# An FFT convolution's last tile: its scratch in four parts instead of three, two of them reloaded early, and 20 filler matmuls instead of 18

## The chip, the core and the metric

The kernel runs on one core of a Trainium2 chip. The metric is the device time of one execution in microseconds, lower is better. The core has five engines with their own instruction streams: TensorE (PE, matmuls; PEld are its weight loads), VectorE (DVE), ScalarE (ACT), GpSimd (POOL) and SyncE (SP), which here only issues transfers. A transfer (DMA) runs on 16 DMA engines beside them and can be issued from SP or from ACT (SPq and ACTq in the profile).

## What is computed

```python
def reference(x, w):                       # x [1, 224, 224, 96], w [7, 7, 96, 96], bf16
    B, H, W, C = x.shape
    K = w.shape[0]
    wp = jnp.pad(w, ((0, H - K), (0, W - K), (0, 0), (0, 0)))
    Xf = rfft2(x.astype(float32), axes=(1, 2))
    Wf = rfft2(wp.astype(float32), axes=(0, 1))
    Yf = jnp.einsum('bhwi,hwio->bhwo', Xf, Wf)
    return irfft2(Yf, s=(H, W), axes=(1, 2)).astype(bfloat16)
```

That is a circular convolution of a 224 x 224 image of 96 channels with a 7 x 7 filter.

## The kernel before

The image is cut along its height into 8 bands of 28 rows (`NJ`, `B`) and along its width into 7 tiles of 32 columns (`t` = 0 to 6; the last is `TL`). Along the height the kernel uses a short transform of 34 points per band, which gives 17 frequencies (`NS`), each with a real and an imaginary part. Every tile goes through three stages, which are interleaved instruction by instruction:

- A: the transform of the columns of the next tile, into `xf` (matmuls pb<-Fm,xn).
- B: for each frequency s = 0 to 16 a round (`b_round`) of matmuls with the transformed filter `WF`, whose results VectorE, ScalarE and GpSimd combine into `yf`. Three frequencies (two at the end) make one group of `yf`, and each group is put to a scratch tensor in DRAM (`scr`), because the next stage needs its rows in another order of partitions. In the last tile the puts of all groups but the last are issued from ACT, one round or so after their sums (`puts`, line 705), the last one from SP.
- C: the inverse transform. The scratch is loaded back with the frequencies of two or three bands on the partitions (`tt`), multiplied with the matrix `G`, evacuated from PSUM to `yo` and written to the output. In the rounds of a tile, jobs of the C stage of the tile before it are interleaved (`c_jobs`, `CQ`, `pace`). Outputs of the next to last tile (except one kind) are kept back in the list `outs` and issued behind the late loads (lines 769 and 984).

After the last tile's rounds there is nothing left to interleave with, so its C stage is cut in two along the frequencies. `SLAST = (0, 9, 15, 17)` (line 37) names the parts. Part 0 (frequencies 0 to 8, tensor `scra`) is loaded back early, in two transfers of 64 and 8 rows at round s = 11 (lines 971 to 975), into `tl_a`, 72 partitions (`KA`). The parts 1 and 2 (frequencies 9 to 14 and 15 to 16, tensors `scrb`) are loaded by `load_b` (line 732) once their puts have landed, 96 and 32 rows of `tl_b`, 128 partitions. Both lie in a buffer of `xf` that is free by then. The matrices for them, `GA` (4 bands at once) and `GB`, are copied together from `G` by small transfers in the tiles 3 and 4 (`g_parts`, line 735; one at each round, line 970).

The end of the kernel (lines 977 to 1016) is then, in program order: the six C jobs left over of tile 5; both `load_b`; the outputs in `outs`; eight early products (`first`, with `GA` and `tl_a`) into the eight PSUM banks; `WARM` = 18 filler matmuls of zeros, which add nothing to the last of these banks (line 1002); then sixteen times a late product (`second`, with `GB` and `tl_b`) onto an early one, its evacuation by VectorE or ScalarE, and after every second an output of 168 KB. The other eight early products follow as banks come free.

SP issues its transfers in program order, and waits in place where a transfer needs something that is not there yet. All helpers record their instructions at one line (L99), so the profile is read by tiles: `xf<-scra` is the early reload, `xf<-scrb` the late loads, `scra<-yf` and `scrb<-yf` the puts of the last tile, `pb<-xf,GA` the early products, `pb<-wu` at the end the fillers, `pb<-xf,GB` the late products.

Of the kernel before, what the change touches and what calls it, by code (L numbers as in the profile page):

```python
# [8 lines left out]
BF16 = mybir.dt.bfloat16  # L9
# [5 lines left out]
B = 28  # L15
# [5 lines left out]
NJ = 8  # L21
# [3 lines left out]
TW = 16  # L25
# [8 lines left out]
PGRP = ((0, 5), (5, 8), (8, 11), (11, 14), (14, 17))  # L34
YGRP = ((0, 3), (3, 6), (6, 9), (9, 12), (12, 15), (15, 17))
YGRPL = ((0, 3), (3, 6), (6, 9), (9, 12), (12, 15), (15, 17))
SLAST = (0, 9, 15, 17)
SA = SLAST[1]
YMAX = 3
YBUF = 4  # L40
JGB = ((0, 3), (3, 6), (6, 9), (9, 12), (12, 15), (15, 17))
# [4 lines left out]
SH3 = (0, 8, 17)  # L46
MERGE = ()
NP2 = 0
WARM = 18
HEAD = ("w",) * 6 + ("x0", "w", "w", "h0", "h1", "w", "w", "x1", "w", "w")  # L50
W1 = 30
ZC = 48
# [12 lines left out]
def kernel(  # L65
# [7 lines left out]
    _, H, W, C = x.shape  # L73
    assert tuple(w.shape) == (KT, KT, C, C) and C == 96 and H == NJ * B and W % (2 * TW) == 0
    NT = W // (2 * TW)
    TL = NT - 1
# [29 lines left out]
    VE, SE, GE, TE, DE = (_Ordered(e) for e in (nc.vector, nc.scalar, nc.gpsimd, nc.tensor, nc.sync))  # L106

    cpool = ctx.enter_context(tc.tile_pool(name="const", bufs=1))
    dr_pool = ctx.enter_context(tc.tile_pool(name="scr", bufs=4, space=bass.MemoryType.DRAM))
# [30 lines left out]
    def tail_evac(out_ap, in_ap, n):  # L140
        cv, ca = 75 + 1.25 * n, 85 + 1.03 * n
        if load["v"] + cv <= load["a"] + ca:
            load["v"] += cv
            return VE.tensor_copy(out=out_ap, in_=in_ap)
        load["a"] += ca
        return SE.copy(out=out_ap, in_=in_ap)

    def dma(out_ap, in_ap):
        return DE.dma_start(out=out_ap, in_=in_ap)
# [7 lines left out]
    G = cpool.tile([3 * FR, 3 * B], BF16, name="Gm")  # L157
    KA = 4 * 2 * SA
    NL = len(SLAST) - 1
    KB = [NJ * 2 * (SLAST[i + 1] - SLAST[i]) for i in range(1, NL)]  # L160
    RB = [sum(KB[:i]) for i in range(NL - 1)]
    assert sum(KB) == 128
    XW = 2 * TW * C
    xn_all = [cpool.tile([128, XW + 32], BF16, name=f"xn{i}") for i in range(2)]
    xn_bufs = [xb[0:R] for xb in xn_all]
# [366 lines left out]
    def a_jobs(t):  # L532
        xf = new_xf(t)
        jobs = []
        for jg in range(2):
            for h in range(2):
                for (q, n) in ((0, 3), (3, 3), (6, 2)):
                    jobs.extend(a_bank(t, xf, xn_bufs[jg], h * PXC + 2 * q, n, jg, HALO + h * 8 + q))
            jobs.append(then_load(jobs.pop(), t + 1, jg))
        return jobs  # L540
# [23 lines left out]
    def jit(t, g):  # L564
        s0, s1 = JGB[g]
        n = s1 - s0
        xf = xf_tiles[t][0:C]
        xv = xf.rearrange("c p r s w j -> c p r s (w j)")
        b = jcount[0] % 3 if t < 2 else (jcount[0] - 2 * len(JGB)) % 2
        jcount[0] += 1  # L570
        Jb = J_bufs[b][0:C].rearrange("c (k s q) -> c k s q", k=7, s=3)
        for s in range(s0, s1):
            jbuf[(t, s)] = Jb[:, :, s - s0]

        def sub(o, a, b, op, cost):
            def f():
                load["v"] += 170 + cost / 1.92
                return VE.tensor_tensor(out=o, in0=a, in1=b, op=op)
            return f
        x0, x1 = xv[:, 0, :, s0:s1], xv[:, 1, :, s0:s1]  # L580
        c0, c1 = max(s0, REAL[0] + 1), min(s1, REAL[1])
        i0, i1 = c0 - s0, c1 - s0
        pd, rd, sd, qd = x1.ap
        dpl = bass.AP(x1.tensor, x1.offset - NJ, [pd, [NJ, 2], rd, sd, qd])
        cuts = ((0, 1), (1, n)) if t == g == 0 else ((0, n),)
        return [
            sub(Jb[:, 0:4, a:b].rearrange("c (k r) s q -> c k r s q", r=2), dpl[:, :, :, a:b],
                x0[:, :, a:b].unsqueeze(1).to_broadcast([C, 2, 2, b - a, PP]), ALU.subtract, 4 * PP * (b - a)) for a, b in cuts] + [
            sub(Jb[:, 4, i0:i1], xv[:, 0, 0, c0:c1], xv[:, 0, 1, c0:c1], ALU.add, PP * (c1 - c0)),
            sub(Jb[:, 5:7, i0:i1], Jb[:, 0:4:2, i0:i1], Jb[:, 1:4:2, i0:i1], ALU.add, 2 * PP * (c1 - c0)),  # L590
        ]
# [13 lines left out]
    def b_round(t, s, mid, end, ydve=False, planes=()):  # L605
# [90 lines left out]
        if s == y1 - 1:  # L696
            dst, yo0 = scr_tiles[t], 0
            if t == TL:
                i = sum(s >= v for v in SLAST[1:])
                dst, yo0 = scr_tiles[(t, i)], SLAST[i]  # L700

# [8 lines left out]
    scr_tiles = {}  # L710
# [18 lines left out]
    tl_a = tl_all[0:KA, 0:2 * TW2].rearrange("p (w g e) -> p w g e", g=2, e=2 * C)  # L729
    tl_b = tl_all[:, 2 * TW2:3 * TW2].rearrange("p (w e) -> p w e", e=2 * C)  # L730

    def load_b(i):
        dma(tl_b[RB[i]:RB[i] + KB[i]], scr_tiles[(TL, 1 + i)].rearrange("w j s (r e) -> (j s r) w e", r=2))

    def g_parts():
        for j in range(4):
            dma(GA[j * 2 * SA:(j + 1) * 2 * SA, j * B:(j + 1) * B], G[0:2 * SA, 0:B])
            yield
        for j in range(NJ):
            for i in range(NL - 1):  # L740
                s, s1 = SLAST[i + 1:i + 3]
                n = 2 * (s1 - s)
                dma(GB[RB[i] + j * n:RB[i] + (j + 1) * n, j // 4, j % 4 * B:(j % 4 + 1) * B], G[2 * s:2 * s1, 0:B])
                yield
# [59 lines left out]
    outs = []  # L804
# [9 lines left out]
    def queue_c(t):  # L814
        pend.extend((t, *k) for k in (LT if t < TL - 1 else LTL))
        pump()
# [33 lines left out]
    def fills(qs, k):  # L850
        def f():
            for q in qs:
                pace(q, k)
        return f
# [3 lines left out]
    def add(a, b, jobs):  # L858
        qs.append([a, b, jobs, len(jobs)])
# [15 lines left out]
    for r in range(NS + LAG):  # L875
# [28 lines left out]
        if r == PGRP[-2][1] + 1:  # L904
# [6 lines left out]
            GA = g_pool.tile([KA, 4 * B], BF16, name="GA")  # L911
            GB = g_pool.tile([128, 2, 4 * B], BF16, name="GB")
# [4 lines left out]
        for t in range(2):  # L917
            s = r - LAG * t
# [11 lines left out]
    if NP2:  # L930
# [3 lines left out]
        pools["ps"], pools["psb"] = (c.__enter__() for c in ps_cms)  # L934
    cj = c_jobs(0)
    gp = g_parts()
    for t in range(2, NT):
        if t == TL:
            scr_tiles[t] = None
            scr_tiles[(t, 0)] = dr_pool.tile([TW, NJ, SA, 4 * C], BF16, name="scra")  # L940
            for i in range(1, NL):
                scr_tiles[(t, i)] = dr_pool.tile([TW, NJ, SLAST[i + 1] - SLAST[i], 4 * C], BF16, name=f"scrb{i}")
        else:
            scr_tiles[t] = dr_pool.tile([TW, NJ, NS, 4 * C], BF16, name="scr")
        qs = []
        if t + 1 < NT:
            add(4 if t == 2 else 0, 26, a_jobs(t + 1))
        nold, nnew = CQ[t]
        k1 = 2 * NS if t < TL else 2 * NS - 8
        k0 = {2: 15, TL: 6}.get(t, 3)  # L950
        km = k0 + -(-(k1 - k0) * nold // (nold + nnew))
        add(k0, km, cj[:nold])
        cn = c_jobs(t - 1)
        cj = cn[nnew:]
        add(km, k1, cn[:nnew])
        plan = {}
        for g, (s0, s1) in enumerate(JGB):
            if g + 1 < len(JGB) or t + 1 < NT:
                plan[s0 if g + 1 < len(JGB) else s0 - 1] = g
        for s in range(NS):  # L960
            now = ()
            if s in plan:
                g = plan[s]
                now = jit(t, g + 1) if g + 1 < len(JGB) else jit(t + 1, 0)
            if s == 2 and t == 2:
                queue_c(0)
            if s == (3 if t in (2, TL) else 2):
                queue_c(t - 1)
            if t in (3, 4):
                next(gp, None)  # L970
            if t == TL and s == SA + 2:
                sv = scr_tiles[(TL, 0)].rearrange("w (g j) s (r e) -> (j s r) (w g) e", g=2, r=2)
                ta = tl_a.rearrange("p w g e -> p (w g) e")
                for p0, p1 in ((0, KA // 16 * 16), (KA // 16 * 16, KA)):
                    dma(ta[p0:p1], sv[p0:p1])
            b_round(t, s, fills(qs, 2 * s), fills(qs, 2 * s + 1), bool(now) if t < TL else s % 3 == 2 or s >= NS - 3, now)
    tail[0] = 1
    load["v"], load["a"] = 1000.0, 0.0
    while cj:
        cj.pop(0)()  # L980
    assert not pend
    for i in range(NL - 1):
        load_b(i)
    for f in outs:
        f()
# [6 lines left out]
    def first(g, q):  # L992
        pc = bank()[0:M4, 0:4 * C]
        TE.matmul(pc.rearrange("p (w e) -> p w e", w=2), lhsT=GA[:], rhs=tl_a[:, 2 * q:2 * q + 2, g], start=True, stop=False)
        return pc

    def second(g, q, pc, yo):
        TE.matmul(pc, lhsT=GB[:, g], rhs=tl_b[:, 2 * q:2 * q + 2, :].rearrange("p w e -> p (w e)"), start=False, stop=True)
        tail_evac(yo[0:M4, q % 4 * 4 * C:(q % 4 + 1) * 4 * C], pc, 4 * C)
    order = [(g, q) for h in range(2) for g in range(2) for q in range(4 * h, 4 * h + 4)]  # L1000
    live = {k: first(*k) for k in order[:8]}
    for _ in range(WARM):
        TE.matmul(live[order[7]].rearrange("p (a b) -> p a b", a=3), lhsT=wu[:, 0:M4], rhs=wu[:].unsqueeze(1).to_broadcast([128, 3, 128]),
                  start=False, stop=False)
# [44 lines left out]
```

## Time and profile before

| What | Value |
|---|---|
| Time, median of 3 runs | 264.14 us (263.65 to 265.39) |
| The profiled execution's own time | 263.5 us |
| Its span, first to last instruction | 261.8 us |
| TensorE busy | 251.5 us (96%) |
| VectorE busy | 220.1 us (84%) |
| ScalarE busy | 196.7 us (75%) |
| GpSimd busy | 97.3 us (37%) |
| Mean granted TensorE clock | 0.992 |

Times inside the profile are microseconds from the span's start. The profile has a page of totals and answers to queries: a chain of work that ended last (from the last instruction back, at each step to what released it), a timeline in order of time (start, duration, engine, output<-input, how many instructions are merged, and in brackets the idle time before and who ended it), lists of waits, and windows (busy time of each engine in a stretch, the granted TensorE clock as a share of full speed, the busy share of the DMA engines and GB/s). Matmuls are pipelined, so a matmul's duration is longer than the distance to the next one's start.

### The profile page before, as it was taken

The numbers are of one execution on the slowest core, as the hardware profiler recorded it, in microseconds if no ns is written. First come the engines' busy times: TensorE is split into PE (matmuls) and PEld (weight loads), VectorE is DVE, ScalarE is ACT, GpSimd is POOL, SyncE is SP. The second block draws the span as 40 slices with busy tenths as digits, with TensorE's granted clock in tenths as the row PEclk, the third lists the DMA queues.
The fourth block names the chain that finished last, engine by engine and source line by source line (L and its number), as shares of the span: only waits on it lengthen the run. The fifth ranks groups of instructions, "written<-read, shape, count | busy, mean of one in ns | idle before, by whom it ended". The sixth has DMA issues, their size and how long they took to land.

```text
span 261.8 us, 11952 instructions
## 1 busy us (share of the span) xinstructions
PE 251.5 (96%) x5046; PEld 232.7 (89%) x5046; DVE 220.1 (84%) x462; ACT 196.7 (75%) x470; POOL 97.3 (37%) x152
## 2 busy tenths in 40 slices
PE   8999999999999999999999999999999999999793
PEld 3979999999989999989999998999999999989561
DVE  6889998899999789868887788788988799999623
ACT  8979978697745967988988799887988852654422
POOL 7783224464655622241223412333134423325000
PEclk9999999999999999999999999999999999999889
DMA  7994105511112698987967496979688442877796
GB/s 177 272 195 126 48 6 155 161 49 48 48 51 85 185 251 155 296 265 192 274 188 218 120 265 207 241 209 357 241 171 248 135 136 87 221 206 212 177 276 195
DMA packets 46889, 46.77 MB, mean 179 GB/s; under 512 B 35308, under 2 KB 38064, under 8 KB 46836
## 3 DMA queue, kind: packets, MB, share of 16 engines
q1 hardware_dynamic: 46116, 44.54, 62.1%
q10 hardware_dynamic: 720, 1.47, 1.7%
q8 instruction: 39, 0.64, 1.1%
q14 instruction: 14, 0.11, 0.1%
HBM read 24.66 MB, written 21.33 MB: 176 GB/s over the span
## 4 chain that ended last, share of the span: by engine, by line
PE 76%; DMA 11%; DVE 8%; issue 2%; ACT 1%; SPq 1%; DVEq 0%; ACTq 0%
PE pb L99 75%; DVE J L99 3%; DMA xn<-in_x_dram 3%; DMA WF<-in_x_dram 3%; DMA xf<-scrb 2%; DVE WF L99 2%; DMA wq<-in_w_dram 2%; DMA scrb<-yf 1%; PE ps L99 1%; DVE v L99 1%; DVE yf L99 1%; DVE u L99 1%; SPq L99 1%; ACT WF L99 0%; DVE tt L99 0%
## 5 line engine op out<-in xcount | busy, mean ns | idle before, releaser
L99 PE MATMUL pb<-WF,J 96*128 96x96 bf16 x2821 | 162.4, 206 | 1.7 <-DVE J L99 0.7
L99 PEld LDWEIGHTS <-J 96*128 96x128 bf16 x2821 | 137.9, 98 | 10.6 <-issue 3.5
L99 POOL TENSOR_TENSOR yf<-v,u 128x384 bf16<-128x384 f32 x70 | 72.5, 1049 | 124.6 <-issue 74.2
L99 ACT CAST xf<-pb 96x408 bf16<-96x408 f32 (+6 forms) x140 | 65.1, 491 | 3.5 <-PE pb L99 1.4
L99 PE MATMUL pb<-WF,xf 96*128 96x96 bf16 x952 | 59.9, 206 | 0.2
L99 DVE TENSOR_TENSOR J<-xf 96x456 bf16<-96x456 bf16 (+3 forms) x85 | 56.0, 697 | 0.0
L99 PEld LDWEIGHTS <-xf 96*128 96x128 bf16 x952 | 47.2, 98 | 1.0 <-PE ps L99 0.6
L99 PE MATMUL pb<-Fm,xn 118*128 118x136 bf16 (+4 forms) x576 | 43.8, 203 | 0.3 <-DMA xn<-in_x_dram 0.3
L99 PE MATMUL pb<-tt,Gm 102*84 102x384 bf16 (+1 forms) x132 | 32.1, 326 | 0.5 <-DVE yf L99 0.5
L99 ACT CAST yo<-pb 84x384 bf16<-84x384 f32 (+1 forms) x61 | 26.2, 483 | 5.7 <-PE pb L99 5.3
L99 PEld LDWEIGHTS <-xn 118*128 118x128 bf16 x576 | 28.6, 97 | 0.5 <-issue 0.5
L99 ACT CAST J<-pb 84x384 bf16<-84x384 f32 (+1 forms) x64 | 27.6, 492 | 0.0
L99 DVE TENSOR_TENSOR J<-J 96x912 bf16<-96x912 bf16 (+2 forms) x42 | 25.3, 603 | 0.0
L99 ACT CAST WF<-pb 96x480 bf16<-96x480 f32 x42 | 21.2, 564 | 0.1
L99 PEld LDWEIGHTS <-wq 128*128 128x128 bf16 (+1 forms) x288 | 19.6, 149 | 0.4 <-issue 0.4
L99 PE MATMUL pb<-wq 128*128 128x120 bf16 x192 | 15.2, 224 | 0.0
L99 DVE TENSOR_TENSOR WF<-WF 96x960 bf16<-96x960 bf16 x15 | 14.0, 932 | 1.4 <-ACT WF L99 1.3
L99 POOL TENSOR_TENSOR yf<-xn,xn 128x384 bf16<-128x384 f32 x9 | 8.8, 997 | 14.8 <-issue 12.1
L99 PEld LDWEIGHTS <-Gm 102*84 102x84 bf16 (+1 forms) x132 | 11.3, 117 | 1.7 <-issue 0.7
L99 DVE TENSOR_TENSOR yf<-v,u 128x384 bf16<-128x384 f32 x20 | 11.6, 579 | 0.7
L99 PEld LDWEIGHTS <-wu 128*128 128x128 bf16 (+1 forms) x41 | 5.7, 142 | 6.0 <-issue 2.5
L99 ACT COPY xf<-xf 96x816 bf16<-96x816 bf16 (+4 forms) x18 | 10.9, 660 | 0.0
(399 smaller groups left out, 265.8 us busy)
## 6 DMA issues: line engine op xcount, KB each, us to landing
scr<-yf SPq DMA_DIRECT2D x30, 288.0 KB
xn<-in_x_dram SPq DMA_DIRECT2D x12, 672.0 KB
tt<-scr SPq DMA_DIRECT2D x24, 336.0 KB
out_dram<-yo SPq DMA_DIRECT2D x12, 252.0 KB
out_dram<-J SPq DMA_DIRECT2D x12, 252.0 KB
tt<-scr SPq DMA_DIRECT2D x6, 288.0 KB
wq<-in_w_dram SPq DMA_DIRECT2D x5, 288.0 KB
WF<-in_x_dram SPq DMA_DIRECT2D x2, 672.0 KB
```

Of the source, the lines that this page charges most:

```text
L99: r = fn(*a, **k)
```

## The change

The last tile's scratch is cut into four parts, `SLAST = (0, 6, 12, 15, 17)`. The first two (`NA` = 2; frequencies 0 to 5 and 6 to 11) are loaded back early, each in one transfer of 48 rows, at the rounds s = 8 and s = 14 (`SREL`). They fill 96 partitions of `tl_a`. Ahead of the second one, the outputs in `outs` are issued. The other two parts (12 to 14 and 15 to 16) are the late ones: 48 and 32 rows, so that `GB` and `tl_b` are used on 80 partitions (`KBS`) instead of 128. `g_parts` has 24 small copies instead of 20. There are 20 fillers instead of 18.

```diff
-SLAST = (0, 9, 15, 17)
-SA = SLAST[1]
+SLAST = (0, 6, 12, 15, 17)
+NA = 2
+SREL = (8, 14)
+SA = SLAST[NA]
...
-WARM = 18
+WARM = 20
...
-    KB = [NJ * 2 * (SLAST[i + 1] - SLAST[i]) for i in range(1, NL)]
-    RB = [sum(KB[:i]) for i in range(NL - 1)]
-    assert sum(KB) == 128
+    KB = [NJ * 2 * (SLAST[i + 1] - SLAST[i]) for i in range(NA, NL)]
+    RB = [sum(KB[:i]) for i in range(NL - NA)]
+    KBS = sum(KB)
+    assert KBS <= 128
...
-        dma(tl_b[RB[i]:RB[i] + KB[i]], scr_tiles[(TL, 1 + i)].rearrange("w j s (r e) -> (j s r) w e", r=2))
+        dma(tl_b[RB[i]:RB[i] + KB[i]], scr_tiles[(TL, NA + i)].rearrange("w j s (r e) -> (j s r) w e", r=2))
...
-        for j in range(4):
-            dma(GA[j * 2 * SA:(j + 1) * 2 * SA, j * B:(j + 1) * B], G[0:2 * SA, 0:B])
-            yield
+        for i in range(NA):
+            s, s1 = SLAST[i:i + 2]
+            for j in range(4):
+                p = 8 * s + j * 2 * (s1 - s)
+                dma(GA[p:p + 2 * (s1 - s), j * B:(j + 1) * B], G[2 * s:2 * s1, 0:B])
+                yield
...
-            if t == TL and s == SA + 2:
-                sv = scr_tiles[(TL, 0)].rearrange("w (g j) s (r e) -> (j s r) (w g) e", g=2, r=2)
-                ta = tl_a.rearrange("p w g e -> p (w g) e")
-                for p0, p1 in ((0, KA // 16 * 16), (KA // 16 * 16, KA)):
-                    dma(ta[p0:p1], sv[p0:p1])
+            if t == TL and s in SREL:
+                i = SREL.index(s)
+                if i == NA - 1:
+                    while outs:
+                        outs.pop(0)()
+                dma(tl_a[8 * SLAST[i]:8 * SLAST[i + 1]].rearrange("p w g e -> p (w g) e"),
+                    scr_tiles[(TL, i)].rearrange("w (g j) s (r e) -> (j s r) (w g) e", g=2, r=2))
...
-    for i in range(NL - 1):
+    for i in range(NL - NA):
         load_b(i)
...
-        TE.matmul(pc, lhsT=GB[:, g], rhs=tl_b[:, 2 * q:2 * q + 2, :].rearrange("p w e -> p (w e)"), start=False, stop=True)
+        TE.matmul(pc, lhsT=GB[0:KBS, g], rhs=tl_b[0:KBS, 2 * q:2 * q + 2, :].rearrange("p w e -> p (w e)"), start=False, stop=True)
```

All four parts' tensors are named `scrb` after the change.

More of the change, by code (lines that the diff above doesn't have):

```diff
@@ L732, in load_b @@
     def load_b(i):
-        dma(tl_b[RB[i]:RB[i] + KB[i]], scr_tiles[(TL, 1 + i)].rearrange("w j s (r e) -> (j s r) w e", r=2))
+        dma(tl_b[RB[i]:RB[i] + KB[i]], scr_tiles[(TL, NA + i)].rearrange("w j s (r e) -> (j s r) w e", r=2))
     def g_parts():
-        for j in range(4):
-            dma(GA[j * 2 * SA:(j + 1) * 2 * SA, j * B:(j + 1) * B], G[0:2 * SA, 0:B])
-            yield
+        for i in range(NA):
[4 more added lines that the diff above has]
+                yield
         for j in range(NJ):
-            for i in range(NL - 1):
-                s, s1 = SLAST[i + 1:i + 3]
+            for i in range(NL - NA):
+                s, s1 = SLAST[NA + i:NA + i + 2]
                 n = 2 * (s1 - s)
@@ L939 @@
             scr_tiles[t] = None
-            scr_tiles[(t, 0)] = dr_pool.tile([TW, NJ, SA, 4 * C], BF16, name="scra")
-            for i in range(1, NL):
+            for i in range(NL):
                 scr_tiles[(t, i)] = dr_pool.tile([TW, NJ, SLAST[i + 1] - SLAST[i], 4 * C], BF16, name=f"scrb{i}")
@@ L981 @@
     assert not pend
-    for i in range(NL - 1):
+    for i in range(NL - NA):
         load_b(i)
```

## The prediction

> **What bounds the kernel now.** I read the chain that ended last first, then TensorE's timeline through the tail, then the DMA issues of SP and ACT, then the windows of one microsecond. The chain, from 225 us on (start, us, what):
>
> ```profile
> 230.66 13.11 PE pb L99 x265
> 243.77 0.56 DVE yf L99
> 244.35 2.97 DMA scrb<-yf
> 247.33 5.48 DMA xf<-scrb
> 252.95 3.96 PE pb L99 x22
> 256.94 0.56 DVE tt L99
> 257.50 0.46 DVEq L1044
> ```
>
> Up to 243.77 TensorE is the bound. Then the last rows are summed, put to scratch (2.97 us) and loaded back (5.48 us); at 252.95 the late products begin. From there to the span's end at 261.8 lie 8.85 us of products, evacuations and output that the change does not touch. So the question is one: when do the late products start? TensorE's own timeline over the same stretch shows that the load is not alone in setting this:
>
> ```profile
> 244.37 0.97 PE L99 MATMUL pb<-tt,Gm 102*84 102x384 bf16 x5 [0.46 <-DVE yf L99]
> 246.32 1.92 PE L99 MATMUL pb<-xf,GA 72*112 72x384 bf16 x8 [0.98 <-DMA xf<-scra]
> 248.04 4.37 PE L99 MATMUL pb<-wu 128*112 128x384 bf16 x18
> 252.95 0.99 PE L99 MATMUL pb<-xf,GB 128*112 128x384 bf16 x5 [0.54 <-DMA xf<-scrb]
> ```
>
> Eight early products wait until 246.32 for the early reload (scra), the 18 fillers follow and end at 252.41, and only the last 0.54 us before 252.95 is a wait for the late load. Whatever makes the late load faster gains at most 0.54 us unless the fillers also end earlier. Now the DMA issues of that stretch (start, time on the issuing queue), where rows 0 to 8 are "scra" and the rest "scrb":
>
> ```profile
> 233.20 0.35 ACTq L99 DMA_DIRECT2D scra<-yf  x1
> ...
> 235.71 0.77 SPq L99 DMA_DIRECT2D out_dram<-yo  x1
> ...
> 237.48 3.04 SPq L99 DMA_DIRECT2D xf<-scra  x2
> ...
> 238.30 0.33 ACTq L99 DMA_DIRECT2D scrb<-yf  x1
> ...
> 242.61 0.33 ACTq L99 DMA_DIRECT2D scrb<-yf  x1
> ...
> 244.35 0.35 SPq L99 DMA_DIRECT2D scrb<-yf  x1
> ...
> 246.87 1.12 SPq L99 DMA_DIRECT2D xf<-scrb  x2
> ```
>
> The put of rows 6-8 (233.20) landed when the reload was released at 237.48: 4.28 us. The put of rows 12-14 (242.61) landed when the first late load was released at 246.87: 4.26 us. The last put took 2.97. These are my prices for a put. The reload issued at 237.48 released the early products at 246.29, though its queue was nearly free at its start. Last, the windows (stretch, busy time of PE, PEld, DVE, ACT, POOL, granted clock, DMA share, GB/s):
>
> ```profile
> 238.00:239.00 1.00, 1.00 (x29) 1.00 (x26) 1.00 (x4) 0.27 (x1) 0.00 (x0) 1.00 0.08 22
> ...
> 247.00:248.00 1.00, 1.00 (x5) 0.69 (x4) 0.00 (x0) 0.00 (x0) 0.00 (x0) 0.61 0.05 13
> 248.00:249.00 1.00, 1.00 (x4) 0.64 (x3) 0.00 (x0) 0.00 (x0) 0.00 (x0) 0.50 0.71 160
> ...
> 250.00:251.00 1.00, 1.00 (x6) 0.72 (x5) 0.00 (x0) 0.00 (x0) 0.00 (x0) 0.69 1.33 213
> 251.00:252.00 1.00, 1.00 (x8) 0.81 (x7) 0.00 (x0) 0.00 (x0) 0.00 (x0) 1.00 1.25 198
> ```
>
> The granted clock is 0.5 from 247.24 to 250.65 (quarter-microsecond windows give 0.93 in 247.00-247.25 and 0.75 in 250.50-250.75). The early products and the fillers run through that stretch.
>
> **How long products and fillers take.** At full clock the alternating GA and GB products start 0.165 us apart (253.94 to 256.41, 15 steps), at half clock 0.33. Check on before: 8+18 of them are 4.29 us of full-clock work. From 246.32 to 247.24 pass 0.92, the half-clock stretch of 3.41 us passes 1.70, the other 1.67 bring it to 252.32; the row says 252.41, so I add 0.09. I use the same sum for after.
>
> **Two more fillers.** 28 instead of 26 is 0.33 us more of full clock: with nothing else moved, the fillers end at 252.74 and the late products start there or so, 0.2 us before 252.95.
>
> **Rows of the matmuls.** Early products have 96 rows instead of 72, late ones 80 instead of 128. The groups by tile have 72 and 128 rows at the same median, 326 ns (weight loads 130 ns both), so this costs and gains nothing; it follows that the 16 evacuations and 8 outputs behind them keep their pace too.
>
> **Bytes of the late load.** 768 KB (576 + 192) become 480 (288 + 192). In the quarter-microsecond windows bytes flow from 247.75 to 252.0, 4.25 us, behind 0.9 us from the issue and before 0.8 us to the landing. At 480/768 the flow is 2.65 us: landing at 251.2 instead of 252.81 if the issues stay at 246.87. If the second of the two (which needs the last put) slips by 1 us, to 248.3, then 0.9+1.06+0.8 give 251.1, hidden; 252.2 is the worst I see. All of this is before the fillers' end, so **the late load stops being the bound and its 1.6 us are not gained**: late next is the chain early reload, 8 products, 20 fillers.
>
> **The first reload (rows 0-5, 576 KB, at s=8).** It needs the put of 227.81, at 2.97 to 4.28 us: 230.8 to 232.1. SP already sat until 232.06, for up to 2.1 us in one wait, on "DMA scra<-yf" in the waits of its queue, so it blocks nothing new. Its issue (0.58 of the two issues' 3.04, or all 3.04) delays what follows on SP: an output and a tt load at 232.06 and 232.49, outputs from 233.23 to 236.48. The tt load feeds the products at 242.57 or later; the outputs feed nobody. SP is free until 237.48 and then again until 244.35, which covers it; without that cover it would cost those 0.6 to 3.0 us. Its bytes need about 3 us of flow, where the windows from 232 to 239 leave about 2.5 us of DMA time unused; the rest runs to about 239.5. ACT's puts of rows 6-8 and 9-11 run beside it.
>
> **The output flushed ahead of the second reload.** One output of 252 KB (its rows are evacuated at 236.95), 0.3 to 1.5 us of SP's queue by the rows of the four such outputs, some 0.7 us of flow, done before 240. It leaves three behind the late loads instead of four, where none is on the chain: nothing.
>
> **The second reload (rows 6-11, 576 KB) is the step that decides.** It needs the put issued at 238.30. By the last put it lands at 241.3, by the busy ones at 242.6. Nearest is the quick one, since the 0.08 share at 238-239 shows the queue emptying; I take 241.3. The reload then takes 0.9 + 576/768 of 4.25 + 0.8 = 4.9 us if alone: 246.2. The put of 242.61 (288 KB) comes in its midst, at 230 GB/s up to 1.28 us: 247.5. I take the middle, 246.85, because half of that put's time falls on the reload's slow first microsecond (160 GB/s at 248-249 in the like load). Ends: TensorE is free at 245.34, so an early landing is worth at most that; the late end is 242.6+4.9+1.28 = 248.8.
>
> What is queued behind its wait on SP: the last put, needed at 244.35. SP is released 3.0 us before (1.7 at the late end), so the wait costs that put nothing; if the issue takes 3.04 us at the late end it slips 1.3 us. Its bytes go behind the reload's, so I let it land up to 1 us later than 247.32, which is the slip counted above.
>
> **Smaller moves.** Four more GA/GB copies on SP at t=3 and 4, 0.75 us each by the rows of those tiles: SP's queue has gaps there and no wait of TensorE in that stretch names it. If that cover went, 3 us of SP delay would meet tt loads issued whole rounds ahead. Clearing GA takes POOL 0.19 us for the same columns: nothing.
>
> **Sum.** Start at 246.85: 0.39 at full clock, 1.70 in the half-clock stretch, 2.53 left of 4.62, end 250.65+2.53+0.09 = 253.27. The late products start then, against 252.95: +0.3 us. The profiled execution took 263.5 (span 261.8, 1.7 around it) and would take 263.8; the median of the three runs is 264.14, 0.64 above the profiled one, so I forecast 264.4. From the ends: start at 245.34 gives 251.76 (-1.2 us, 262.9), at 248.8 gives 254.45 (+1.5 us, 265.6). Break-even is a start at 246.5.
>
> **The rivals.**
> 1. *The reload is early.* The second reload goes as one transfer of 48 rows; before, an issue of 64 rows and one of 8 took 8.8 us together. If it is landed when the tail's own products end (245.34), the start is 251.8: 262.9. For it: the put's queue is empty and the slow small issue is gone. Against it: 241.3+4.9 is already 246.2 without any other transfer. 0.14.
> 2. *The clock stays up.* If no half-clock stretch came, the products and fillers would take 28 x 0.165 = 4.62 from 246.85, to 251.5, beside the landing at 251.2: -1.45 us, 262.7. Against it: the same gap of TensorE, 243.9 to 246.3 with 0.97 us of work in it, preceded the drop at 247.24, and mine is as long. 0.10. [...]
> 3. *Slower: the put of rows 9-11 lands late.* Place: SP's wait at the second reload. Price: the first reload's and the output's bytes stand before that put, it lands at 242.6, the reload at 248.8, the late products at 254.45, +1.5 us, 265.6. It decides once the reload lands after 246.5. For it: two of three prices of a put are 4.3. Against it: 238-239 is nearly empty now. 0.18, of it 0.07 beyond 1% (that would need a landing near 251, as if SP stood behind one more transfer).
>    [...]
>
> **How the numbers follow.** My forecast (start between 252.6 and 253.8, so 263.8 to 265.0) has 0.58, the rivals 0.14, 0.10 and 0.18. The range from 262.9 to 265.6 leaves out most of rival 2 and the tail of rival 3. One per cent is 2.6 us, about what a measurement of this kernel can tell from no change. Faster by more would need late products before 250.3, ahead of the late load's landing at 251.2: 0.03. Slower by more: 0.08. Within: 0.89.
>
> **What would show it.** Right: no wait for scrb before the late products, which follow the 20th filler at once; the late load landed a microsecond or more earlier; the early products released by scrb's or scra's reload between 246.2 and 247.5; the half clock still 3.4 us long. Wrong: a wait for the late load still ends last (then the last put or SP was held up); the fillers at full clock throughout; or early products after 248, with the last put issued after 244.7.

## The result, and the profile after

The changed kernel takes 267.42 us (median of 6 runs, 265.97 to 269.11) beside 264.03 us for the kernel before (6 runs). The ratio is 1.0117, 95% interval [1.007, 1.0165]: slower, by 3.4 us in the medians (1.2 to 1.3%). Here and below the ratios leave out executions more than 1.5% above the fastest of the same kernel and the medians do not, so the two need not agree to the last digit. The forecast was 264.4 us, 262.9 to 265.6. The profiled execution took 267.54 us, span 265.8.

The chain that ended last, from where the last tile's puts enter it (start, us, what):

```profile
237.00 1.03 DVE yf L101
...
238.09 6.29 DMA scrb<-yf
...
244.44 5.07 DMA xf<-scrb
...
249.64 11.55 PE pb L101 x50
...
261.21 0.56 DVE tt L101
```

Before, the chain ran through the last put and the late load. Now it runs through the put of rows 9-11 (issued at 238.09, landed 6.29 us later) and the second early reload (5.07 us). The late load is not in it. TensorE's timeline in the tail:

```profile
244.17 0.97 PE L101 MATMUL pb<-tt,Gm 102*84 102x384 bf16 x5 [0.18 <-DVE yf L101]
249.64 2.78 PE L101 MATMUL pb<-xf,GA 96*112 96x384 bf16 x8 [4.50 <-DMA xf<-scrb]
252.21 5.19 PE L101 MATMUL pb<-wu 128*112 128x384 bf16 x20
257.24 0.98 PE L101 MATMUL pb<-xf,GB 80*112 80x384 bf16 x5
```

TensorE waits 4.50 us for the second reload (before: 0.98 for the early one), the early products start at 249.64 instead of 246.32, and the late products follow the fillers without any wait, at 257.24 instead of 252.95. That is 4.3 us; the two profiled executions differ by 4.0. What SP issued meanwhile (start, time on the queue):

```profile
233.26 0.32 SPq L101 DMA_DIRECT2D tt<-scr  x1
233.63 1.08 SPq L101 DMA_DIRECT2D xf<-scrb  x1
234.81 3.43 SPq L101 DMA_DIRECT2D out_dram<-J  x3
238.34 1.24 SPq L101 DMA_DIRECT2D out_dram<-yo  x2
244.44 0.33 SPq L101 DMA_DIRECT2D xf<-scrb  x1
244.82 0.94 SPq L101 DMA_DIRECT2D scrb<-yf  x1
246.96 3.46 SPq L101 DMA_DIRECT2D xf<-scrb  x2
```

The first reload goes out at 233.63 behind a tt load, the second at 244.44, and the last put, ready near 244.1, at 244.82. In the windows (stretch, busy time of the five engines, clock, DMA share, GB/s) two things stand out:

```profile
238.00:239.00 1.00, 1.00 (x29) 1.00 (x26) 1.00 (x4) 0.39 (x1) 0.00 (x0) 1.00 1.37 128
239.00:240.00 1.00, 1.00 (x28) 1.00 (x26) 1.00 (x4) 0.02 (x1) 0.05 (x1) 1.00 1.40 127
240.00:241.00 1.00, 1.00 (x29) 1.00 (x26) 1.00 (x4) 0.41 (x1) 1.00 (x2) 1.00 1.37 131
...
254.00:255.00 1.00, 1.00 (x5) 0.68 (x4) 0.00 (x0) 0.00 (x0) 0.00 (x0) 0.50 0.54 197
255.00:256.00 1.00, 1.00 (x5) 0.67 (x4) 0.00 (x0) 0.00 (x0) 0.00 (x0) 0.60 0.00 0
256.00:257.00 1.00, 1.00 (x8) 0.81 (x7) 0.00 (x0) 0.00 (x0) 0.00 (x0) 1.00 0.00 0
```

First, while the put of rows 9-11 should be flowing, the DMA engines are busy (share 1.4) and yet move only 130 GB/s; before, a share of 1.33 moved 213. By the packet records of the trace (start, length and size of every DMA packet) these are the 384-byte packets of the first reload, at 65 ns each, where the other reloads' mostly take 22 to 40; they last until 241.75, and nearly all of the put's packets come after them, up to 245.5 together with those of the next put. The first of them goes only at 240.2, 2.1 us after the issue. Second, the half clock lasts from 248.98 to 255.81, twice as long as before.

### The profile page after: what moved, and what is told of

Read it like the earlier page. It is cut to its first block, busy times and chain, and to the rows that moved or that the text cites. A ratio compares the mean times of both kernels' runs of the same rounds, so it can differ in the third digit from the quotient of the medians.

```text
span 265.8 us, 11965 instructions
## 1 busy us (share of the span) xinstructions
PE 253.5 (95%) x5048; PEld 234.2 (88%) x5048; DVE 219.6 (83%) x462; ACT 196.8 (74%) x470; POOL 97.4 (37%) x152
## 4 chain that ended last, share of the span: by engine, by line
PE 79%; DVE 8%; DMA 7%; issue 2%; ACT 2%; DVEq 0%; SPq 0%; ACTq 0%
PE pb L101 73%; PE ps L101 6%; DVE J L101 4%; DMA xn<-in_x_dram 3%; DMA scrb<-yf 2%; DMA xf<-scrb 2%; DVE xn L101 1%; DVE yf L101 1%; DVE WF L101 1%; DVE v L101 1%; ACT WF L101 1%; DVE u L101 0%; DVE tt L101 0%; ACT xf L101 0%; DVEq L1051 0%
## 5 line engine op out<-in xcount | busy, mean ns | idle before, releaser
L101 DVE CAST tt<-pb 112x384 bf16<-112x384 f32 x8 | 4.2, 556 | 11.6 <-PE pb L101 11.2
L101 ACT CAST tt<-pb 112x384 bf16<-112x384 f32 x8 | 3.5, 481 | 12.6 <-PE pb L101 12.5
L101 PEld LDWEIGHTS <-wu 128*128 128x128 bf16 (+1 forms) x43 | 6.5, 155 | 6.9 <-issue 3.6
```

The source lines that it names most:

```text
L101: r = fn(*a, **k)
```

## The experiments

Theory 1: the first reload's bytes stand before the put of rows 9-11, that put lands late, and the second reload behind it. Rival (theory 2): the flushed output stands there. Later theory 1b: the first reload is slow because of the partitions it is written to. The kernel before took 264.10 us when measured beside e1 to e4, 263.81 beside e5 to e8 and 263.91 beside e9 to e11; each ratio below is to the one measured beside it. The changed kernel was not measured again beside them, so differences to its 267.42 us go across these groups, between which the kernel before itself moves by 0.3 us.

**e1: no first reload.** All else as changed. The kernel then lacks the load of rows 0-5 of the last tile and multiplies stale rows in their place, so the last columns of its output are not the convolution's.

```diff
-                dma(tl_a[8 * SLAST[i]:8 * SLAST[i + 1]]..., scr_tiles[(TL, i)]...)
+                if i:
+                    dma(tl_a[8 * SLAST[i]:8 * SLAST[i + 1]]..., scr_tiles[(TL, i)]...)
```

> Leaves out the first early reload (rows 0-5), so the output's last columns use stale rows there. Theory 1 (the first reload's 576 KB stand before the put of rows 9-11): that put lands by 241.3 instead of 244.4, the second reload is issued there and lands near 246.3, the late products start near 253.0, time about 264.3. Theory 2 (the flushed output of 252 KB is what stands before it): the put still lands after 243.5 and the time stays above 266.5.

Measured: 263.28 us, ratio to before 0.9948 [0.9914, 0.9982]. Its chain and one window:

```profile
238.18 3.87 DMA scrb<-yf
...
242.06 5.55 DMA xf<-scrb
...
247.75 10.19 PE pb L101 x50
```

```profile
238.00:239.00 1.00, 1.00 (x29) 1.00 (x26) 1.00 (x4) 0.31 (x1) 0.00 (x0) 1.00 0.45 143
```

The same put, issued at the same time, lands after 3.87 us instead of 6.29, and the queue is half empty at 238. It is 0.8 us later than theory 1 had it (242.06 for 241.3), but the whole loss is gone: theory 1 holds. (The profiled execution took 264.26 us, 1 us more than the median. Its half clock lasted 3.41 us, so part of the gain comes from the clock: see the point on the clock below.)

**e2: no flush.** The outputs stay behind the late loads.

```diff
-                if i == NA - 1:
-                    while outs:
-                        outs.pop(0)()
```

> The outputs kept back are not issued ahead of the second reload but behind the late loads, as before the change. Theory 1: the put of rows 9-11 still lands after 243.5, because the first reload's packets are done only near 241.7; time 266.5 to 267.5. Theory 2: the put lands by 242, time 264 to 265.5.

Measured: 268.14 us, 1.0102 [1.0061, 1.0143]. The put of rows 9-11 and the second reload in the trace:

```profile
237.90 0.33 ACTq L101 DMA_DIRECT2D scrb<-yf  x1
244.55 0.33 SPq L101 DMA_DIRECT2D xf<-scrb  x1
```

The put issued at 237.90 released the second reload at 244.55, 6.65 us later. Theory 2 falls.

**e3: the first reload one round earlier.**

```diff
-SREL = (8, 14)
+SREL = (7, 14)
```

> The first reload one round earlier (s = 7), so that SP need not issue it behind the tt load that waits for a buffer until 233.3. Theory 1 (place): it is issued near 232, flows in the hole of 232.5 to 233.7 and is done by 238, the put of rows 9-11 lands by 242 and the time falls to 264 to 265.5. Rival (its packets take 65 ns each wherever they stand, 4.5 us for 576 KB): they last until about 240, the put lands near 242.5, time about 266.

Measured: 267.25 us, 1.0088 [1.0054, 1.0122], and a miss as a test: SP's order of issues did not change (output, tt load, first reload at 234.16), because nothing else is issued on SP between the two places. Where the reload stands cannot be moved by this number.

**e4: the two early reloads swap their partitions.** Rows 0-5 to partitions 48-95, rows 6-11 to 0-47 (GA alike).

```diff
-                dma(tl_a[8 * SLAST[i]:8 * SLAST[i + 1]]...
+                dma(tl_a[48 - 8 * SLAST[i]:96 - 8 * SLAST[i]]...
```

> The two early reloads swap their partitions: rows 0-5 go to partitions 48 to 95, rows 6-11 to 0 to 47. If the 65 ns of a packet come from the destination partitions 0 to 47, the first reload's packets now take about 25 ns (done by 239.5, time near 264.5) and the second's 65 (landing 2 to 3 us later after its issue than the 5.1 us of the changed kernel). If they come from what runs beside or from the source, nothing moves: 267.4.

Measured: 268.43 us, 1.0118 [1.0057, 1.0179]. The windows in which the first reload flows, and the chain:

```profile
239.00:240.00 1.00, 1.00 (x28) 1.00 (x26) 1.00 (x3) 0.15 (x1) 0.14 (x1) 1.00 1.18 199
240.00:241.00 1.00, 1.00 (x29) 1.00 (x26) 1.00 (x3) 0.41 (x1) 0.00 (x0) 1.00 1.29 199
```

```profile
239.64 4.88 DMA scrb<-yf
244.58 6.81 DMA xf<-scrb
251.53 11.31 PE pb L101 x50
```

In these windows the first reload now moves at 200 GB/s instead of 130 (36 to 41 ns a packet), the put lands after 4.88 us, and the second reload, now into partitions 0 to 47, takes 6.81 us instead of 5.07. So the destination partitions matter: they changed, and the rows, the source and the order did not. They are not the whole cause: in its new place the reload into 0 to 47 moved at 207, 171 and 152 GB/s in the windows from 246 to 249 (the one of the change at 204, 289 and 272; in both the late load joins in from about 247), not at 130. Its expectation was missed in size: packets near 25 ns and 264.5 us were expected, and what the first reload gained the second one lost. (All of the last rounds lie 1.5 us later in this execution, so its times of the clock are not to be laid beside those of the others; durations are.)

**e5: 6 fillers.**

```diff
-WARM = 20
+WARM = 6
```

> Changes one term: 6 fillers instead of 20. If the late products wait for the fillers and not for the late load (landed 252.8 in the changed kernel, fillers to 257.2), they start near 254.3: 249.6 + 2.6 for 8 products at half clock + 6 x 0.33, and the time falls by about 2.5 us to 264.9. The first late products then run at half clock until about 255.6. Rival: the clock matters more than the wait, the late products run at half clock longer, and less than 1 us is won.

Measured: 265.34 us, 2.1 us less than the change; 1.0018 [0.9978, 1.0057].

```profile
250.10 2.78 PE L101 MATMUL pb<-xf,GA 96*112 96x384 bf16 x8 [4.70 <-DMA xf<-scrb]
252.68 2.13 PE L101 MATMUL pb<-wu 128*112 128x384 bf16 x6
254.59 1.72 PE L101 MATMUL pb<-xf,GB 80*112 80x384 bf16 x5
```

The late products start at once behind the sixth filler, at 254.59 instead of 257.24, although the second reload was 0.5 us later here. So the fillers are what the late products wait for, not the late load.

**e6: even and odd partitions.** Rows 0-5 go to the even partitions of 0 to 95, rows 6-11 to the odd ones (GA alike).

```diff
-                dma(tl_a[8 * SLAST[i]:8 * SLAST[i + 1]]...
+                dma(tl_a[i:KA:2]...
```

> The first early reload goes to the even partitions of 0 to 95, the second to the odd ones; sizes, times of issue and everything else as changed. Theory 1b (the first reload is slow because its 48 rows lie in partitions 0 to 47, which share few ways into SBUF): its packets take 25 to 40 ns instead of 65, DMA moves about 250 GB/s instead of 130 between 237 and 240, it is done by 239.7, the put of rows 9-11 lands by 242.3 and the second reload by 247.7; time 264.5 to 265.5. Rival (576 KB at that place are slow because of what runs beside, or because of 3 rows per engine): packets stay at 65 ns, time 267 or more. [...]

Measured: 265.42 us, 2.0 us less than the change; 1.0067 [1.0041, 1.0092].

```profile
238.00:239.00 1.00, 1.00 (x28) 1.00 (x26) 0.96 (x2) 0.53 (x2) 0.69 (x1) 1.00 1.34 261
239.00:240.00 1.00, 1.00 (x29) 1.00 (x26) 1.00 (x4) 0.30 (x1) 0.00 (x0) 1.00 1.08 205
240.00:241.00 1.00, 1.00 (x28) 1.00 (x26) 1.00 (x4) 0.11 (x1) 0.00 (x0) 1.00 1.01 354
```

```profile
239.18 4.16 DMA scrb<-yf
243.40 5.54 DMA xf<-scrb
249.07 10.20 PE pb L101 x50
```

Same bytes, same size, same place in the queue: 261 GB/s in the first of these windows, packets at 32 to 38 ns in the first two. By the packet records all but the last 2% of the reload are through in 3.0 us (237.1 to 240.1), in the change in 4.3 (237.3 to 241.65). The put lands after 4.16 us. In this execution it was issued 1.1 us later than in the change (239.18 for 238.09), so it met less of the reload; by the clock it lands 1.0 us earlier, at 243.34. Theory 1b holds by these flows. The time alone would not settle it, since its interval and that of the change (1.007 to 1.0165) overlap. It is not all: without the reload (e1) the put takes 3.87 and the time is 2.1 us lower still.

**e7: e6 with the late loads spread too.** `RB = [KB[1], 0]`: the 48 rows in partitions 32-79, the 32 rows in 0-31.

> As e6_even_odd, and the late loads are placed so that the 32 rows of the last part lie in partitions 0 to 31 and the 48 rows of the part before in 32 to 79. Theory 1b: the late loads land up to 1 us earlier than in e6, but the fillers hide that: time equal to e6 within 0.5 us. Rival (the late load bounds): a further 0.5 us or more.

Measured: 265.65 us, 1.0052 [1.0014, 1.0091], as e6: the late load is hidden behind the fillers. This execution had the half clock for 6.83 us, as the change had, and e6 only for 3.41; so e7 is the fairer one beside the change.

```profile
238.41 4.45 DMA scrb<-yf
```

```profile
255.66 0.98 PE L101 MATMUL pb<-xf,GB 80*112 80x384 bf16 x5
```

Its put took 4.45 us instead of 6.29, and its late products start at 255.66 instead of 257.24, 1.6 us earlier with as much half clock.

**e8 and e11: the kernel before, its early reload spread.** Partitions 32-95 and 96-103 instead of 0-63 and 64-71; GA is zero below.

```diff
-    KA = 4 * 2 * SA
+    KA = 32 + 4 * 2 * SA
...
-                for p0, p1 in ((0, KA // 16 * 16), (KA // 16 * 16, KA)):
-                    dma(ta[p0:p1], sv[p0:p1])
+                for p0, p1 in ((0, 64), (64, KA - 32)):
+                    dma(ta[32 + p0:32 + p1], sv[p0:p1])
```

> The kernel before, with its early reload in partitions 32 to 95 and 96 to 103 instead of 0 to 63 and 64 to 71 (the rows below are multiplied by zero). Theory 1b: the 64 rows spread over twice the ways, the reload lands 1.5 to 2 us earlier, the put of rows 9-11 too, the early products start near 245.4 when TensorE is free; the late load then bounds at 252 to 252.8: 263.3 to 264.1. Rival: the reload lands at 246.2 as before, 264.1.

> e8_before_spread again, for its interval beside the two others. If the 1.2 us of e8 stand, 262.4 to 263.0 and below the kernel before; if they were noise, 263.5 to 264.2.

Measured: 262.62 us, 0.9967 [0.9932, 1.0002], and again 263.77 us, 0.9973 [0.9941, 1.0005]. e8 came out below the 263.3 to 264.1 us expected of it, and e11, the same kernel, inside the 263.5 to 264.2 named for noise. The mechanism shows (e8's trace), the gain stays inconclusive:

```profile
245.89 1.48 PE L99 MATMUL pb<-xf,GA 104*112 104x384 bf16 x8 [0.68 <-ACT yo L99]
247.21 3.09 PE L99 MATMUL pb<-wu 128*112 128x384 bf16 x18
252.04 0.99 PE L99 MATMUL pb<-xf,GB 128*112 128x384 bf16 x5 [1.75 <-DMA xf<-scrb]
```

The early products no longer wait for their reload but for an evacuation (0.68), and now the late load bounds, with 1.75 us of wait.

**e9: four parts with 9, 3, 3 and 2 rows.** `SLAST = (0, 9, 12, 15, 17)`, `SREL = (11, 14)`, the first reload in partitions 32-103, the second (24 rows) in 0-23, no flush, `WARM = 10`.

> What the earlier runs point to: parts 0-8, 9-11, 12-14, 15-16. Rows 0-8 are reloaded at s = 11 as before the change, but into partitions 32 to 103; rows 9-11 at s = 14 in 24 rows of partitions 0 to 23; the late loads have 480 KB; outputs are not flushed ahead; 10 fillers. Only 288 KB instead of 576 then wait for the put of rows 9-11 and nothing new stands before that put. If this is right, that put lands near 243.3, the second reload near 246.8, the late load near 250.8 and the late products start between 250.8 and 251.5: 261.5 to 262.3. Rival (any reload behind that put comes too late): second reload after 248, late products after 252.5, 263.5 or more.

Measured: 264.54 us, 1.0028 [1.0006, 1.005], a miss. The put of rows 9-11 took 5.80 us (238.17 to 244.03 in the chain), and by the packet records only 5 of its 128 packets went before 241: the 72-row reload issued just before it stands in its way as the 48-row one did; the second reload released the early products only at 248.88.

**e10: e7 without the flush and with 6 fillers.**

> e7_all_spread with the outputs behind the late loads as before and 6 fillers. The put of rows 9-11 lands near 242.8, the second reload near 248, late load 251.3; 8 products at half clock and 6 fillers end near 252.6, so 262.8 to 263.5. Rival (half clock through the late products costs what the fillers saved): 264 or more.

Measured: 263.63 us, 0.9982 [0.9955, 1.001], just above the 262.8 to 263.5 expected: 3.8 us below the change and not to be told from the kernel before. No version tried here that loads all rows clearly beats the kernel before.

## Why the prediction was wrong, point by point

- **The deciding step was named, and its price was wrong; so was the clock behind it.** "The put of rows 9-11 lands at 241.3" failed: it landed at 244.4. Its worst price there, 4.28 us, was taken from other puts in the kernel before; it took 6.29. Break-even was a landing of the reload at 246.5; it landed at 249.5. This is rival 3 by place and mechanism, with a larger size: 1.5 us were forecast for it, and beyond 1% it had 0.07. The sign named for being wrong came: early products after 248 (249.64) with the last put issued after 244.7 (244.82).
- **What made it late is the first reload, which I had priced as harmless** ("its bytes need about 3 us of flow, the rest runs to about 239.5"). Two parts of that failed. It was issued at 233.63, behind an output (232.83) and a tt load (233.26) that the prediction put after it, not by 232.1, and its packets came behind those of the 336 KB tt load, from about 237.25. And its flow took 4.5 us, not 3: I scaled by bytes from the late load, whose first 96 rows lie in partitions 0 to 95. The nearest row would have been the early reload of the kernel before, 64 rows in partitions 0 to 63, 768 KB. e1 prices the whole at 4.1 us (267.42 to 263.28), the clock that goes with it included. The medians of e6 and e7 put the crowding in partitions 0-47 at 1.8 to 2.0 of them (267.42 to 265.65 and 265.42); as the intervals overlap that of the change, this size is an estimate, and e7's trace, 1.6 us, is the better one.
- **My reading of the quiet window was wrong.** I took the DMA share of 0.08 at 238-239 as the state that the put of 238.30 would meet. In the kernel before that put too landed late, at 243.7 by the trace's semaphore records, after 5.4 us; nothing waited for it until after 246, so no view of waits shows it. The change made something wait for it. Its first packet went only at 241.15 (packet records), 2.85 us after its issue, although the engines were half empty in the window before too:

```profile
239.00:240.00 1.00, 1.00 (x28) 1.00 (x26) 1.00 (x4) 0.22 (x2) 0.00 (x0) 1.00 0.55 97
```

So an empty queue does not show that a put's packets go; in e1, with no first reload, they began 1.0 us after the issue.
- **Right:** the second reload after its issue, 4.9 us forecast if alone (5.55 with half of the put of 242.61 in its midst), 5.07 measured. The flush costs nothing (e2). The late load stops being the bound and its gain is lost (e5, e7). The products and fillers by the sum: from 249.64 at half clock to 255.81 is 3.08 us of 4.62, the rest ends at 257.35; the row says 257.24.
- **The clock.** I took a stretch of 3.41 us at half clock; it lasted 6.83 us, after 4.5 us of waiting. The clock records of the traces give 3.413 us before and 6.827 us after, twice as long; what sets that length no run shows. The clock term is the larger part of the miss. The prediction's own sum, with the measured start of 249.64 put in and the clock left as forecast, gives 254.9; the row says 257.24. So of the 4.0 us between the forecast 253.27 and the row, 1.6 are the late start and 2.4 the clock: about 0.9 because the stretch began at 248.98 instead of 247.24, and 1.5 because it lasted twice as long (3.41 us would have ended the fillers at about 255.7, an estimate by the same sum). The longer stretch seems the rule after the change (the mean clock also counts half clock behind the last product): of its six executions five had a mean granted clock of 0.981 to 0.987 (the profiled one 0.987) and one, the fastest (265.97 us), 0.991. Within one kernel the difference shows too: e7's six executions at 0.987 took 265.5 to 267.2 us, its four at 0.991 to 0.994 264.3 to 265.4. In e1's trace, of the 3.3 us by which the late products start earlier (253.99 for 257.24), 1.9 are the earlier start of the early products (247.75) and 1.4 the shorter half-clock stretch (3.41 us). What decides between 3.41 and 6.83 us stays open. The length of TensorE's wait alone does not: e2's trace has a wait of 4.38 us and 3.41 us of half clock, e7's a wait of 2.70 us and 6.83.
- **SP's wait delayed the last put** by 0.7 us at most (issued at 244.82, ready near 244.1), hidden by the fillers as forecast.

Still open: why the put on ACT's queue got almost no packets through while SP's queue carried the reload (in the change the first went 2.1 us after the issue and nearly all came as the reload's ended, at 241.75; in e9 5 of 128 went before 241), whether that lies in the issue or in the engines. That the reload's packets are slow cannot be all of it: in e9 the reload ran at 300 GB/s from 240 to 241 with packets of 22 ns, and the put still waited. In the kernel before and in e9, where the reload was issued about a microsecond before the put, the put's first packet came 2.85 and 2.55 us after its issue with the engines about half busy or less (shares of 0.08 to 0.60 from 238 to 240). That speaks for the issue rather than full engines there, but no run tests it. Issuing the first reload ahead of the tt load that it follows was not tried.

## What to carry to other kernels

A transfer that nobody waits for has no visible price (in the kernel before, 5.4 us of a put that no view of waits shows); before a change makes something wait for it, look at what flows beside it and when its own packets go, not at how empty the queue looks when it is issued (a share of 0.08 there, and the first packet 2.85 us after the issue). Bytes moved earlier are not free when they land in front of the next link of the chain (4.1 us here by e1, the clock included). Price a load into few partitions by rows of the trace with the same partitions, not by its bytes alone (4.5 us of flow here, where the bytes alone had 3), and recount fillers whenever the transfer that they cover gets shorter or what starts them gets later (6 instead of 20 took 2.1 us off, e5).

## What the runs showed of the hardware

In the windows shown, the same 48 rows of 12 KB flow at about 130 GB/s into partitions 0 to 47, at about 200 into 48 to 95 (e4), and at up to 261 when spread over the even partitions of 0 to 95 (e6); the packets take 65 ns, 36 to 41 and 32 to 38. The 130 is no fixed rate of those partitions: in e4 the second reload ran into them at 152 to 207 GB/s, and the early reload of the kernel before, into 0 to 63, at 262 GB/s in 240-241. So the rate follows neither from the bytes nor from the partitions alone. Why the placement moves the flow no run shows; the ways into SBUF in the expectations of e6 and e8 were my assumption, and what the runs showed is the flow by placement, the 130, 200 and 261 GB/s above. The half clock in the tail began at 247.2 before, at 249.0 after and in e11 only at 254.5, in the late products; e8, the same kernel as e11, had none there. Where it fell ahead of the last products, it lasted 3.41 us in the traces of before, e1, e2 and e6, and 6.83 us in those of after and e7. So one profile of this tail tells its times only to about a microsecond; that the intervals of e8 and e11 stay open for the same reason is likely, but not shown.
